# K projection of the last two chunks of layer 2 by Strassen, with its sums in free units of the h buffer

## The chip, the cores and the metric

The kernel runs on one core of one Trainium2 chip. The metric is the device time of one execution in microseconds; lower is better. The comparison uses the median of several executions.

## The reference

Four layers over a sequence of 2048 tokens of width 512: linear attention, feed-forward, linear attention, feed-forward, each with a layer norm in front and a residual behind. Both attention layers share their weights, and so do both feed-forward layers.

```python
def _A_ref(x, wqkv, wo):            # H = 32 heads of 16
    qkv = (x @ wqkv).reshape(B, S, 3, H, Dh).transpose(2, 0, 3, 1, 4)
    q, k, v = qkv[0], qkv[1], qkv[2]
    phi = lambda t: jnp.where(t > 0, t + 1, jnp.exp(t)) + 1e-6
    pq, pk = phi(q), phi(k)
    kv = jnp.einsum("bhsd,bhse->bhde", pk, v)
    z = jnp.einsum("bhsd->bhd", pk)
    num = jnp.einsum("bhqd,bhde->bhqe", pq, kv)
    den = jnp.einsum("bhqd,bhd->bhq", pq, z)[..., None] + 1e-6
    return (num / den).transpose(0, 2, 1, 3).reshape(B, S, D) @ wo

def _B_ref(x, w1, w2):              # Dff = 1376
    return jnp.maximum(x @ w1, 0) @ w2

x = x + _A_ref(_layernorm(x), wqkv, wo)
x = x + _B_ref(_layernorm(x), w1, w2)
x = x + _A_ref(_layernorm(x), wqkv, wo)
x = x + _B_ref(_layernorm(x), w1, w2)
```

## The kernel before

**Tiles and layers.** The sequence lies in 16 tiles of 128 tokens, and four tiles make a chunk, so there are chunks 0 to 3. The layers are numbered 0 to 3; layers 0 and 2 are attention, 1 and 3 feed-forward. `xn` holds the normed rows, `Tb` their transposes, which a DMA transpose on SP's queue (`tr8`, `tr10` and so on, two tiles each) writes from `xn`. `big` is one buffer of 44 units of 512 columns: in the feed-forward layers it holds the hidden activations h (unit `h_unit(c, t)`, 11 column blocks c for each chunk t), in the attention layers the phi of K (blocks 0 to 3) and of Q (blocks 4 to 7). Blocks 8 to 10 are not used by attention.

**Attention.** For each tile i, `kproj`i makes K with four matmuls of 512 columns; `a_k_proj` (line 590) sends the result through phi: two passes of ACT out of PSUM (`_lin`, `_exp`) and two of DVE (`_em`, `_phi`). `gacc`i then adds xn^T times phi(K) to an accumulator in four PSUM banks, `z`i the sums for the denominator. `qproj`t_j makes Q by column blocks of 128. `den`, `ln`, `rd` give the reciprocal denominators, which a DMA round trip spreads over the rows of `xn`; `us` multiplies them into phi(Q). `kvT`, `kvm`, `wp`, `wpe` make the small weight from the accumulator (copied out by `gev`), and `wo` the layer's output, which `resid` adds to the rows; `cen`, `sq` and the transposes lead to the feed-forward.

**Feed-forward.** Chunks 1 to 3 make h by one level of Strassen (products p1 to p7); the output products f1 to f7 and `fr` do so too, with the sums s1 to s4 of h on DVE. `q21`, `q22`, `r11`, `r12` pass partial results between those products, `residf` adds the output to the rows and sums them, `sq` (ACT) sums the squares, `mean`, `nm2`, `var`, `veps` (DVE), `rstd` (POOL) and `nbias` (DVE) make the norm's factors, `norm` (DVE or ACT) writes `xn`, `tr` transposes it into `Tb`.

**Strassen for Q.** In layer 2, chunk 3's Q is made by `a_str` (line 711): 512 tokens, 512 inputs and 512 outputs are halved each, and seven products of four 256-column matmuls take the place of sixteen 512-column matmuls. It needs five differences of weight blocks (`waq_0` to `waq_4`, line 686, in rows 8 to 12 of `xin`), four sums of blocks of `Tb` (`tb0` to `tb3`, line 703, in the chunk's own rows of `xn`), and between the products copies and additions of PSUM banks: `c6`, `c11`, `c12` (lines 747 and 748, ACT or DVE) and `c21`, `c22` (DVE). The products p1, p6 come first; p2 and p5 wait for c11, p3 and p4 for c21, p7 for c12.

**Order.** Nothing is scheduled on the chip. The program builds a list of operations with their dependences, and the table `ORDER` gives the order in which they are put into the engines' queues, with a letter that fixes the engine where there is a choice (a for ACT, d for DVE). `BANKS` gives each result's PSUM bank. Each engine works through its queue in order, and waits where an operand isn't there. So an operation that waits holds up everything behind it on its engine.

Of the kernel before, what the change touches and what calls it, by code (L numbers as in the profile page):

```python
# [9 lines left out]
F32 = mybir.dt.float32  # L10
# [123 lines left out]
49 37 45 50 73 38 46d 72 51 81 74 39a 75 52 54 82 76 53a 60 83 86 58 78 56 87 77 79 61 57 55 98 59 89 62 84 63 119 88  # L134
93 99 115 100 108 64 66d 95 65d 67a 103 80 69 117 68a 92 85 90 94 113 70 135 105 91 104 116 120 141 114 118 121 110
180 122 109 251 174 130 176 123 136 132 127d 124d 131 125d 142 138 126d 128 178 137 148 143 179 133 181 129 175 144
169 177 134 182 149 96 183 106 159 111 171 112 170 97 147 107 160 101 161 184 191 185d 186a 187d 139 164 140 150 189
172 192 153 173 165 151 239 188d 193 154 102 190 166 145 162 203 155 163 167 156 9 152 209 194 10 205 157 195 11 204
197 146 210 158 196 206 199 207 198 240 221 200 168 211 201 215 223 212 213 222 233 224 217 225 216 227 218 234 219
235 202 428 228 208 229 236 237 252 230 231 253 427 254 214 255 322 282 323 242 220 283 243 226 324 241 284 232 325  # L140
245 285 238 244 246 326 250 247 259a 329 248 249 257d 256a 260 286 258a 287 270 262 327 289 261 280 263 328 330 272
264 288 271 265 281 290 314 267 273 320 291 275 315a 333 331 321a 318 268 316 277 319d 294 317a 332 266 309 293 274
296 292 395 311 269 278 310 297 400 396 295 276 397 410 401 398a 279 405 402 411 403a 339 412 406 413a 415 334 407 340
408a 383 335 343 349 416 341 336 338 337d 344 350 342a 299 351 353 345 354 384 429d 304 346 352d 301 347d 433 300 424
355 434 436a 465 430d 306 466 449 425 435a 450 305 426 437 468a 438 385 356 298 421 312 451a 431d 386 470 348 432d 469
369 471d 439a 302 422d 399 371 307 423 303 404 377 372d 467a 414 389 440 363 388 378a 308 442 390 364a 313 441 472 387
443a 357 481 370d 444a 473 474 417 409 358 375 359 445 475a 476a 447 446 418 482 393 373 477 376a 392 365 483 394 448d
374a 484 367 452a 391 478 366a 419 498 368d 420 493 499 486 502 503 494 487 500 497 508 485 501d 495 488 504 496a 381
509 507 513 379 510 512 490 505 506d 479 511a 454 491 453 489 382a 514 515 360 380a 492 456 480a 519 361a 545d 455a
524 362 520 529 525 523 546d 566 528 534 567a 530 549 533 547d 458 550a 548d 603 459a 457 604a 598d 568 460a 599d 551  # L150
569 602 552 570 461 553 571 605a 463 554 572 462 464a 601d 555 535 573a 618 556a 674d 538 607 578 526 608a 675d 561
527a 600d 606 521 621d 522a 562 609 579 539 563 677d 557 574 564 580 558 581 565 678 559 575 679a 622 582 576 680 560
623 681 634 536 624a 583 682 637d 577 537d 610 683 638 613a 611 584 531 585 532d 639 612a 684 586 676d 540 587 640a
616 685a 614 695 617a 619 588 751d 696a 595 591d 620a 615 592a 697 625 690 596a 698 594 589a 627 516 590d 626 628a
752d 635 593 699 754d 636a 753d 629a 686 700 691 630 597 701 641 632 702a 631 642 517 541 633a 643 518 542 687 644d
692 707 645a 693 703 646 694 648 647 708 649a 688 755 803d 689 662 758a 804d 756 664 772 757a 805d 704 759 773a 709
806d 663 760 807 761a 705 650 808a 762 706 771 710 652 763 651 774d 809 711 712 764 766d 775 765a 810 769 665 713 811
770a 714 715 666 716 776 812 656 777a 778 717 813 719a 720d 780 814d 658 779 543 767 544 718a 819 653 781d 824 782a
722 787 654 657 815 783 825a 785 659 668 790d 786a 721d 792 768 670 723 791 793d 826 669 784 660 816 748 827 817 828
749a 671 818 788 829 724 750 789d 794 830 726 672 796 725 831d 795 820 797d 798a 727 832 728 836 799 837 800 801 730  # L160
802a 873d 736 732 731 874d 821 833 738 838 655 737 875d 877 876d 661 822 667 834 878a 823 839 879 835 894 880 840 673
895d 841 842 843 881 733 844 734 845 896 882 729 897 739 846 898 849d 850a 848d 883 847d 852 735 899 884d 900 740 851
1066 889 1065 890 1068 1067 885 901d 891 902 892 886 903 893 887 742 904 888 906 744 907 743 908 745 868 905 909 746
910 741 911 912 1069 869 747 913 914 870 915 858 871 872 943 916 860 920d 853 859 919d 861 922 958 855 862 918d 854
863 917d 959 856 921 960 944 857 865 948 961 864 962 953 866 950 867 949 933 951 954 952 955 968 935 956 934 928 957
936 937 969 930 929 923 931 932 938 924 925 945 939 970 926 940 927 963 941 942 980 965 964 946 966 982 971 967 981
947 983 972 984 985 973 995 974 987 975 1000 986 988 997 1001 989 996 1070 998 990 999 1071 978 1002 992 976 991 979
1005 993 1004 1072 1025a 977 1006 994 1003 1024a 1027 1023d 1026a 1073 1011 1029 1009 1047 1028 1030 1007 1012 1074
1048 1075 1077a 1010 1049 1013 1076d 1051 1078 1050a 1008 1053 1014 1055 1031 1054a 1032 1052d 1056d 1037 1034 1084
1033 1133 1039 1035 1015 1036 1038 1123 1017 1134 1018 1135 1118 1124 1016 1136a 1040 1128 1127 1125 1119 1126a 1019  # L170
1085 1120 1129 1042 1121a 1130 1022 1091a 1086 1138 1021 1044 1079 1020 1131d 1097 1043 1045 1182 1087 1139 1041 1046
1081 1167 1183 1080 1088 1184 1057 1168 1098 1172 1099 1169 1170d 1177 1058 1173 1137 1174 1147 1175d 1059 1100 1187
1082 1122 1149 1089 1090 1148a 1178 1159 1132 1060 1150d 1185a 1155 1179 1101 1180a 1083 1161 1092 1156a 1188 1196d
1151 1093 1162d 1094 1216 1189 1140 1152a 1063 1141 1200 1095 1171 1062 1096 1157 1142 1061 1203d 1160a 1143 1064
1219d 1106 1158a 1153 1107 1197d 1176 1163 1199d 1104 1154a 1165 1103 1108 1164d 1181 1201 1109 1102 1166a 1144 1105
1198d 1202a 1204 1300d 1186 1205 1207 1220 1145a 1232 1206a 1111 1193 1302d 1113 1235a 1217 1301d 1194a 1110 1208
1218a 1112 1209 1303d 1195 1236 1210a 1221 1223 1319 1222a 1146 1190 1248 1191 1117 1211a 1192 1115 1225 1114 1212
1224 1226a 1214 1116 1320a 1253 1213 1215a 1249 1321 1227a 1250 1251d 1237 1252 1258 1322 1254 1238a 1230 1255 1257
1323 1256d 1259 1231a 1263 1268 1324 1262 1304 1260 1264 1325 1265 1267 1261d 1233 1279 1305d 1326a 1266d 1234a 1228
1306 1269 1327 1307 1239 1330 1338d 1308 1280 1331 1309 1283 1241 1229 1240 1242d 1310 1243a 1281 1282a 1339d 1274  # L180
1311d 1244 1342 1275 1246 1343 1247a 1340d 1315 1345a 1245 1341d 1344a 1284 1390d 1278 1312 1285 1316 1391d 1288 1347
1276 1346 1392d 1277a 1358 1328 1349 1348a 1317 1294 1313 1332 1393d 1361a 1350 1351 1286 1333 1363 1352a 1362 1270
1364a 1271 1287d 1394 1353a 1272 1318 1273 1359 1329 1356 1360a 1289 1428d 1395a 1365 1357a 1396 1290 1366 1354 1335
1369a 1293 1397 1367 1291 1374 1336a 1292d 1398 1355 1368a 1295 1296 1372 1399 1375 1370 1377a 1400 1373a 1337 1379
1376d 1401a 1409 1371 1380a 1297 1405 1298 1314 1410a 1299 1402 1432 1411 1334 1429d 1435a 1431d 1378 1433 1412 1406
1430d 1434a 1413 1381 1437 1414 1382 1438a 1383 1415 1384a 1385d 1436 1416a 1386 1465 1403 1466a 1407 1387 1449 1404
1448 1450a 1439 1388 1420 1389a 1408 1451a 1421 1480d 1441 1440 1442a 1482d 1452 1443a 1464 1481d 1453 1467a 1417
1454a 1444 1446 1484 1447a 1445 1455 1422 1469 1485a 1468 1483d 1470a 1457 1418 1458a 1423 1499 1486 1471 1500a 1419
1456 1473 1487 1501 1424 1459a 1472 1474a 1502 1488 1460 1425 1461 1475a 1503 1489 1426a 1476 1462 1427 1490 1477
1463a 1504 1478 1517d 1491a 1505 1479a 1495 1506a 1515d 1496 1510 1516d 1497 1511 1498 1519 1518d 1534 1520a 1507  # L190
1535a 1521 1536 1522 1508 1537 1512 1523 1509 1538 1524 1492 1539 1513 1525 1540 1526a 1493 1541a 1530 1494 1527 1514
1528 1542 1529 1543 1545 1554 1544 1546 1531 1547 1555 1532 1548 1549 1533 1550 1551 1553 1552
"""
BANKS = ("0143601322754564754755774454754476476457623555746335427175640021331757302711647524361554634572435036"
# [1263 lines left out]
```

## Time and profile before

| | us |
|---|---|
| median of 5 runs | 271.37 |
| lowest, highest | 271.18, 271.56 |
| profiled execution | 271.37 |
| its span | 269.6 |
| PE, DVE, ACT busy in it | 263.1, 232.7, 196.0 |

The span runs from the first to the last instruction of the program; the profiled execution's time is 1.8 us longer. PE is the TensorE matmul, PEld the weight load beside it, DVE the VectorE, ACT the ScalarE, POOL the GpSimd, SP the SyncE that issues most DMAs. In a timeline each line has a start, a length, the engine, the source line, the operation with what it writes and reads, and, in brackets, idle time before it with what ended it. Line 539 is a helper that issues nearly all matmuls, so they are told apart by their operands: `ps<-wqkv,Tb` is a kproj, `ps<-Tb,wqkv` a qproj, `ps<-big,xn` a gacc, `ps<-gw,big` a wo, `ps<-xn,wqkv`, `ps<-xn,xin` and `ps<-Tb,xin` of 256 columns around 180 us are Q's Strassen products. The matmuls' ends are modelled, so rates are read from start to start. In the chain that ended last, each line has a start, a length and what the end of the execution waited for in that time.

### The profile page before, as it was taken

The numbers are of one execution on the slowest core, as the hardware profiler recorded it, in microseconds if no ns is written. First come the engines' busy times: TensorE is split into PE (matmuls) and PEld (weight loads), VectorE is DVE, ScalarE is ACT, GpSimd is POOL, SyncE is SP. The second block draws the span as 40 slices with busy tenths as digits, with TensorE's granted clock in tenths as the row PEclk, the third lists the DMA queues.
The fourth block names the chain that finished last, engine by engine and source line by source line (L and its number), as shares of the span: only waits on it lengthen the run. The fifth ranks groups of instructions, "written<-read, shape, count | busy, mean of one in ns | idle before, by whom it ended". The sixth has DMA issues, their size and how long they took to land.

```text
span 269.6 us, 5295 instructions
## 1 busy us (share of the span) xinstructions
PE 263.1 (98%) x1951; PEld 170.9 (63%) x1973; DVE 232.7 (86%) x635; ACT 196.0 (73%) x426; POOL 18.8 (7%) x30
## 2 busy tenths in 40 slices
PE   8999999999999999999999999999999999999995
PEld 2444454447556879778666544455458678888884
DVE  4999985999989999999799765599989999979875
ACT  3889956999978768787542887799998857657420
POOL 4111000000110002111010100000011001100000
PEclk9999999999999999999999999999999999999999
DMA  6954973254344026204004060215355222220204
GB/s 216 376 111 79 236 263 103 91 77 102 97 121 76 2 40 97 42 1 80 19 2 78 0 81 1 72 54 127 82 139 118 41 39 41 58 81 0 100 0 156
DMA packets 47481, 23.60 MB, mean 88 GB/s; under 512 B 36736, under 2 KB 46048, under 8 KB 47456
## 3 DMA queue, kind: packets, MB, share of 16 engines
q1 hardware_dynamic: 47312, 23.21, 35.1%
q8 instruction: 15, 0.25, 0.4%
q14 instruction: 10, 0.08, 0.1%
q10 hardware_dynamic: 144, 0.07, 0.1%
HBM read 11.21 MB, written 3.15 MB: 53 GB/s over the span
## 4 chain that ended last, share of the span: by engine, by line
PE 86%; DVE 9%; DMA 2%; issue 1%; ACT 1%
PE ps L539 84%; DVE bst L446 3%; DMA Tb<-xn 2%; PE ps L423 2%; DVE big L525 1%; DVE xn L478 1%; DVE xn L579 1%; DVE escr L523 1%; DVE mv L447 0%; PE ps L502 0%; DVE xin L1055 0%; ACT sqscr L546 0%; DVE escr L1055 0%; DVE xres L552 0%; DVE ps L1029 0%
## 5 line engine op out<-in xcount | busy, mean ns | idle before, releaser
L521 ACT ACTIVATE escr<-ps 128x512 bf16<-128x512 f32 x60 | 35.7, 606 | 8.0 <-PE ps L539 8.0
L546 ACT ACTIVATE sqscr<-xres 128x512 bf16<-128x512 f32 x48 | 30.4, 634 | 14.5 <-DVE xres L583 7.6
L519 ACT ACTIVATE big<-ps 128x512 bf16<-128x512 f32 x60 | 35.2, 608 | 1.0 <-PE ps L539 1.0
L1015 ACT ACTIVATE big<-ps 128x512 bf16<-128x512 f32 (+1 forms) x47 | 24.9, 536 | 9.6 <-PE ps L539 8.9
L539 PE MATMUL ps<-wqkv,Tb 128*128 128x512 bf16 x121 | 30.1, 379 | 1.2 <-DMA Tb<-xn 0.7
L539 PE MATMUL ps<-big,xn 128*128 128x512 bf16 x123 | 29.8, 379 | 0.3
L539 PE MATMUL ps<-gw,big 128*128 128x512 bf16 x120 | 28.7, 379 | 0.5
L539 PE MATMUL ps<-Tb,wqkv 128*128 128x512 bf16 x112 | 27.0, 379 | 0.1
L525 DVE TENSOR_TENSOR big<-big,escr 128x512 bf16<-128x512 bf16 x60 | 24.6, 421 | 2.4 <-ACT big L519 1.5
L523 DVE TENSOR_SCALAR escr<-escr 128x512 bf16<-128x512 bf16 x60 | 16.9, 288 | 9.5 <-ACT escr L521 9.0
L539 PE MATMUL ps<-w2s,big 128*128 128x256 f16 x160 | 21.9, 273 | 0.0
L539 PEld LDWEIGHTS ps<-wqkv,Tb 128*128 128x128 bf16 x128 | 12.0, 98 | 14.7 <-DMA Tb<-xn 1.2
L539 PEld LDWEIGHTS ps<-big,xn 128*128 128x128 bf16 x128 | 12.2, 98 | 13.7 <-issue 0.4
L539 PE MATMUL ps<-w,big 128*128 128x256 f16 (+2 forms) x113 | 20.6, 302 | 0.0
L539 PEld LDWEIGHTS ps<-gw,big 128*128 128x128 bf16 x128 | 12.2, 98 | 12.8 <-issue 0.5
L539 PE MATMUL ps<-w,xin 128*128 128x256 bf16 (+1 forms) x140 | 19.5, 273 | 0.0
L539 PE MATMUL ps<-xn,xin 128*128 128x256 f16 x128 | 19.5, 272 | 0.0
L998 ACT ACTIVATE ps<-ps 128x512 f32<-128x512 f32 (+1 forms) x28 | 14.6, 522 | 5.7 <-DVE big L1036 2.5
L539 PEld LDWEIGHTS ps<-Tb,wqkv 128*128 128x128 bf16 x112 | 10.8, 98 | 12.5 <-issue 0.2
L539 PE MATMUL ps<-xn,w 128*128 128x256 f16 x120 | 18.7, 273 | 0.0
L539 PE MATMUL ps<-Tb,w 128*128 128x512 bf16 x80 | 18.4, 379 | 0.0
L539 PE MATMUL ps<-Tb,wper 128*128 128x256 bf16 x120 | 18.3, 273 | 0.0
(152 smaller groups left out, 513.0 us busy)
## 6 DMA issues: line engine op xcount, KB each, us to landing
xn<-rdram SPq DMA_DIRECT2D x32, 128.0 KB
wqkv<-in_A_wqkv_dram SPq DMA_DIRECT2D x3, 512.0 KB, 7.2
xin<-in_A_x_dram SPq DMA_DIRECT2D x3, 512.0 KB, 8.0
out_dram<-xn SPq DMA_DIRECT2D x3, 512.0 KB, 2.6
w<-in_B_w_dram SPq DMA_DIRECT2D x1, 1376.0 KB, 6.4
w<-in_B_w_dram SPq DMA_DIRECT2D x1, 1280.0 KB, 9.8
rdram<-rsp SPq DMA_DIRECT2D x8, 128.0 KB, 1.7
wo<-in_A_wo_dram SPq DMA_DIRECT2D x1, 512.0 KB, 10.1
```

What stands on the lines that cost most here:

```text
L423: last = e.matmul(psv[:, wt, :], wrm[:, 0:128], wrm[:, :], start=True, stop=True)
L446: g.add(DVE, lambda e: e.bn_stats(bst[:, i, :], xin[:, i, :]), [("xin", i)] + list(behind), [("bst", i)], C_DVE_BNST, name="bnst%d" % i)
L478: (DVE, lambda e: e.tensor_scalar(xn[:, i, :], src, rstd[:, i:i + 1], nbias[:, i:i + 1], ALU.mult, ALU.add), C_DVE_NORM_BF if first else 4 ...
L519: g.add(ACT, lambda e: e.activation(dst_ap, psv[:, b, :], ACTF.Identity, bias=1.0 + 1e-6, scale=1.0), [("ps", b)], [dst_key], C_ACT_PSUM, ...
L521: g.add(ACT, lambda e: e.activation(escr[:, s, :], psv[:, b, :], ACTF.Exp), [("ps", b)], [("escr", s)], C_ACT_EXP, name=name + "_exp")
L523: g.add(DVE, lambda e: e.tensor_scalar(escr[:, s, :], escr[:, s, :], 1.0, 1e-6, ALU.min, ALU.add), [("escr", s)], [("escr", s)], C_DVE_BF4 ...
L525: g.add(DVE, lambda e: e.tensor_tensor(dst_ap, dst_ap, escr[:, s, :], ALU.max), [dst_key, ("escr", s)], [dst_key], 340.0, name=name + "_phi")
L539: last = e.matmul(o, l, r, start=st, stop=sp, skip_group_check=skip)
L546: g.add(ACT, lambda e: e.activation(sqscr[:, q, :], xres[:, i, :], ACTF.Square, accum_out=dst[:, i:i + 1]), [("xres", i)], [("sqscr", q), ...
L579: g.add(DVE, lambda e: e.scalar_tensor_tensor(xn[:, i, :], psv[:, b, :], rstdf[:, i:i + 1], xres[:, i, :], ALU.mult, ALU.add), rd, [("xn", ...
L998: g.add_flex([(ACT, lambda e: e.activation(dst(), psv[:, src, 0:W], ACTF.Identity), cost(C_ACT_PSUM)), (DVE, lambda e: e.tensor_copy(dst() ...
L1015: g.add_flex([(ACT, lambda e: e.activation(out_ap(r, m), pv(b), ACTF.Relu), cost(C_ACT_PSUM)), (DVE, lambda e: e.tensor_scalar(out_ap(r, m ...
```

## The change

K of chunks 2 and 3 of layer 2 is made by `a_str` as well (14 products in place of 8 groups of kproj). The five differences of K's weights lie in blocks 8 to 10 of `big` at chunks 0 and 1, the intermediate of c6 in blocks 8 and 9 at chunk 2, and the sums of `Tb` in the units that later take phi(Q) of the same chunk, because `xn` is still read by gacc. The differences are made new for each layer that needs them. The sums of `Tb` are no longer shared between kinds, so chunk 3 makes them twice, once for K and once for Q. The PSUM copies and additions are written as two halves of 256 columns for both kinds, since K's intermediate lies in two units.

`ORDER` and `BANKS` are new. The list grows from 1556 to 1585 operations; about twenty operations of other layers change between DVE and ACT, trev1 in the head and, at the end of layer 1, norm8 and norm13 to norm15 among them, and matmul groups stand in another order from the first layer on.

```diff
 17 0 14 12 15 18 13 1 16 19 2 20 22 3 24 4 21 23 25 5 6 26 27 7 28 8 29 40 30 33 31 32a 41 34 47 42 35 71 43 36 48 44
-49 37 45 50 73 38 46d 72 51 81 74 39a 75 52 54 82 76 53a 60 83 86 58 78 56 87 77 79 61 57 55 98 59 89 62 84 63 119 88
+49 37 45 50 73 38 46d 72 51 81 74 39d 75 52 82 56 76 53a 54 86 83 60 78 87 55 58 77 61 57 98 59 79 89 62 84 63 119 88
...
-                 ... QSTR=(3,), UACT=(), KSTR=(), GSPLIT=(15,), ...
+                 ... QSTR=(3,), UACT=(), KSTR=[(), (2, 3)], GSPLIT=(15,), ...
...
-        WSUM = {"q": 8, "k": 0}
...
         def qk_weight_sums(kind):
-            if kind in qk_sums:
-                return qk_sums[kind]
+            tag = kind, cur_layer[0]
+            if tag in qk_sums:
+                return qk_sums[tag]
...
-                i = WSUM[kind] + k
-                ap = xin[:, i, :].bitcast(F16).rearrange("p (c f) -> p c f", c=2)
-                keys = [("qks", kind, k), ("xin", i)]
+                if kind == "q":
+                    ap, own = xin[:, 8 + k, :], ("xin", 8 + k)
+                else:
+                    u = h_unit(8 + k % 3, k // 3)
+                    ap, own = unit_ap(u), ("big", u)
+                ap = ap.bitcast(F16).rearrange("p (c f) -> p c f", c=2)
+                keys = [("qks", kind, k), own]
...
-        def t_sums(t):
-            if t in t_sums_of:
-                return t_sums_of[t]
-            TS = [xn[:, 4 * t + k, :].bitcast(F16).rearrange("p (i c t) -> p i c t", c=2, t=128) for k in range(4)]
-            tk = [[("ts", t, k), ("xn", 4 * t + k)] for k in range(4)]
+        def t_sums(t, kind):
+            tag = t, kind, cur_layer[0]
+            if tag in t_sums_of:
+                return t_sums_of[tag]
+            home = [xn[:, 4 * t + k, :] if kind == "q" else unit_ap(pq_unit(k, t)) for k in range(4)]
+            TS = [x.bitcast(F16).rearrange("p (i c t) -> p i c t", c=2, t=128) for x in home]
+            tk = [[("ts", kind, t, k), ("xn", 4 * t + k) if kind == "q" else ("big", pq_unit(k, t))] for k in range(4)]
...
-            s6 = xin[:, 13:15, :].rearrange("p a b -> p (a b)").bitcast(F32)
-            k6 = [("xin", 13), ("xin", 14)]
+            if kind == "q":
+                s6 = xin[:, 13:15, :].rearrange("p a b -> p (a b)").bitcast(F32).rearrange("p (j k) -> p j k", k=256)
+                k6 = [("xin", 13), ("xin", 14)]
+            else:
+                s6 = big[:].bitcast(F32).rearrange("p (c t k) -> p c t k", t=NCH, k=256)[:, 8:10, 2, :]
+                k6 = [("big", h_unit(8, 2)), ("big", h_unit(9, 2))]
...
-                g.add_flex([(ACT, lambda e: e.activation(dst(), psv[:, src, :], ACTF.Identity), C_ACT_PSUM),
-                            (DVE, lambda e: e.tensor_copy(dst(), psv[:, src, :]), C_DVE_FLEX)],
+                g.add_flex([(ACT, lambda e: e.activation(dst(), pv(src), ACTF.Identity), C_ACT_PSUM),
+                            (DVE, lambda e: e.tensor_copy(dst(), pv(src)), C_DVE_FLEX)],
...
-                        if layer == 2 and t in KSTR:
+                        if t in KSTR[layer // 2]:
                             if i % 4 == 0:
                                 a_str(t, "k")
```

In the names of the prediction, `kp1_2` is K's product p1 of chunk 2 (p for product, and so on to `kp7_3`), `kc11_2` its copy c11, `wak_0` to `wak_4` the differences of K's weights, and `tb0_2`, `tb0_3` the sums of `Tb`.

## Prediction

> **What bounds the kernel now.** I read the page first, then the windows around the end of layer 1, then the chain that ended last, then the timelines of PE and DVE there.
>
> ```profile
> PE 263.1 (98%) x1951; PEld 170.9 (63%) x1973; DVE 232.7 (86%) x635; ACT 196.0 (73%) x426; POOL 18.8 (7%) x30
> PEclk9999999999999999999999999999999999999999
> PE 86%; DVE 9%; DMA 2%; issue 1%; ACT 1%
> ```
>
> PE is busy in 263.1 of 269.6 us at full granted clock, and 86% of the chain is PE. Of its 6.5 us of idle time most lies in the head and behind the last matmul. So a microsecond of matmul taken out anywhere in the middle is worth a microsecond, as long as PE finds its operands as early as before. That second condition is what this change strains, so I read the place where it acts.
>
> ```profile
> 135.00:150.00 15.00, 14.85 (x104) 9.87 (x104) 13.53 (x39) 6.24 (x17) 1.17 (x1) 1.00 0.19 36
> 150.00:160.00 10.00, 9.29 (x71) 4.51 (x71) 8.11 (x27) 8.22 (x19) 1.01 (x1) 1.00 0.46 55
> 160.00:168.00 8.00, 7.87 (x65) 4.03 (x65) 3.90 (x13) 5.79 (x12) 0.00 (x0) 1.00 0.00 1
> 168.00:178.00 10.00, 9.88 (x66) 4.97 (x66) 6.57 (x19) 8.34 (x17) 0.00 (x0) 1.00 0.20 67
> ```
>
> Columns: length, busy time of PE, PEld, DVE, ACT, POOL, clock, DMA. From 150 to 178 us DVE is idle for 9.4 us and ACT for 5.7; from 135 to 150 DVE has only 1.5 us left and ACT 8.8. The chain leaves PE in exactly one place of the middle:
>
> ```profile
> 149.53 0.04 DVE xres L583
> ...
> 150.32 0.72 ACT sqscr L546 x2
> ...
> 152.91 1.00 DVE xn L478 x2
> 153.91 0.03 DVE escr L523
> 153.94 4.74 DMA Tb<-xn
> 158.68 0.05 issue
> 158.72 3.84 PE ps L539 x17
> ```
>
> This is layer norm of chunk 3 between the layers: the last residual (residf13), its squares, the norm, the DMA transpose tr14, then kproj14. It takes 9.15 us from 149.53 to 158.68, and the work left for PE does not quite cover it:
>
> ```profile
> 156.18 1.89 PE L539 MATMUL ps<-Tb,wqkv 128*128 128x512 bf16 x8
> 158.72 1.04 PE L539 MATMUL ps<-wqkv,Tb 128*128 128x512 bf16 x4 [0.66 <-DMA Tb<-xn]
> ...
> 160.46 1.03 PE L539 MATMUL ps<-wqkv,Tb 128*128 128x512 bf16 x4
> 161.32 1.03 PE L539 MATMUL ps<-big,xn 128*128 128x512 bf16 x4
> ...
> 185.58 0.60 PE L539 MATMUL ps<-xn,xin 128*128 128x256 f16 x4
> 186.02 1.04 PE L539 MATMUL ps<-Tb,xin 128*128 128x256 bf16 x8
> ```
>
> PE idles 0.66 us before kproj14. The lines also give rates, from start to start: four matmuls of 512 columns (a kproj, qproj or gacc) take 0.86 us (160.46 to 161.32), one Strassen product of four 256-column matmuls takes 0.44 (185.58 to 186.02).
>
> **PE.** Over long runs the rates are finer: 24 matmuls of 512 columns from 190.78 to 195.96, 0.216 us each; ten of 256 columns from 139.72 to 140.81, 0.109 each. A chunk of K was 16 x 0.216 = 3.45 us and becomes 28 x 0.109 = 3.05. Two chunks: 0.80 us less, all of it on the path.
>
> The Trainium skill ("TensorE: Matmul & The Clock Gate", section "Back-to-back issue gap") speaks against the change: in a real stream with weight loads it gives about 81 ns per matmul at 128 columns and 131 at 512. A straight line between them is 98 ns at 256, and by that estimate a chunk would go from 2.10 to 2.75 us, 1.3 us lost over both. Weight loads (98 ns in the groups) do stay below 109 ns here and PE never runs a 512-column matmul in 131, so I use the rows.
>
> **DVE and ACT.** Added on DVE: five differences of K's weights (wak; four of Q's run from 144.24 to 145.58, 0.34 each), eight sums of T (tb, 0.34 in sequence), four additions out of PSUM (c21, c22, 0.69), one of six copies (0.69). Four norms of 0.46 (norm8, norm13 to norm15) move from DVE to ACT. That is 1.7 + 2.7 + 2.8 + 0.7 - 1.8 = 6.1 us. ACT gets five copies at 0.49 in sequence and four norms at 0.71: 5.3 us. The phi work is the same, eight pairs of ACT passes. Both sums fit under the idle times above, so I cost them at nothing as throughput; their cover is the 9.4 and 5.7 us, and if it went they would cost what exceeds it. What can hurt is position, since DVE and ACT run in order.
>
> **Position, before the transposes.** In the new order wak_1, waq_0 and wak_3 stand on DVE among the r11, q22, norm and residf steps of the last output pairs. Walking that queue with the durations above from s4_3 on, the four residuals come back to back, and residf13 starts about 0.5 us after its product fr0_13 is done, where it was 0.04. Behind it tb0_2 and wak_2 lie in the time that the squares of sq13 take anyway (var3 waits for them, 150.32 to 151.04). From nbias3 to the first transpose the new order (norm12 on DVE beside norm13 on ACT) takes about 1.0 us where two norms on DVE took 1.2. On SP's queue tr12 now goes before tr14, and POOL's rstd stands where it stood. Then kp1_3 needs tb0_3 behind the transpose: 0.42 and 0.05. So the chain from fr0_13 to kp1_3 is 0.5 + 9.15 - 0.2 + 0.47 = 9.9 us.
>
> The cover: between fr0_13 and kp1_3 the new order has gacc0 to gacc6 and the seven products of chunk 2, 7 x 0.86 + 7 x 0.44 = 9.1 us, where the old one had 8.6 (149.49 to 158.06). In there kp1_2 itself waits for tb0_2 behind residf13, by the same walk 0.2 us. So PE waits 9.9 - 9.1 - 0.2 = 0.6 at kp1_3, if the transpose again takes 4.74. The transposes of this trace go from 3.0 to 4.8 us (tr8 and tr10, the pair before, 3.1 and 3.2), unlike on equal work; with 3.2 the wait is nothing. I take the middle, 0.3: waits of 0.5 together where 0.66 was, 0.15 gained. Ends: 0.2 and 0.8, so 0.5 gained to 0.15 lost.
>
> **Position, the links.** In each chunk p2 and p5 wait for the copy c11, p4 and p3 for c21 (which waits for c6), p7 for c12. A link is 0.6 to 0.7 us of work and about 0.2 to see the matmuls end. PE work standing in each in the new order: chunk 2: kp6 and gacc2 (1.3), kp5, gacc3 and gacc4 (2.2), kp3 and gacc5 (1.3); chunk 3: gacc7 and kp6 (1.3), qproj0_1 (0.86), kp3 and three z sums (1.7). The thin one is qproj0_1. The Q chunk of the same form ran at 176.84 to 187.05 with no wait over 0.14. Behind the waiting DVE steps stand phi passes, for which gacc8 and later wait only microseconds afterwards. I take 0.1 for the links; ends 0 and 0.9.
>
> **The rest of the table.** About twenty engine choices swap between DVE and ACT in other layers; PE's list elsewhere has the same matmuls. Three spots I looked at. In the head trev1 moves to DVE, whose chain from 9.6 to 24 us is full: 0.35 us later transposes for chunk 2 of layer 0, but two more Q groups (1.7 us) stand before the K matmuls that need them, so nothing; 0.3 without that cover. At kvT, gev0 now follows the last gacc with two Q products (0.87) against 0.89 of need, at wo1 the copies wpe end about when PE arrives: 0.1 together, and the old 0.14 at wp1 goes. The tail has the same steps in another order. I take 0.15 for all; ends -0.2 and 0.6.
>
> **Sum.** The profiled execution took 271.37 us (span 269.6 and 1.8 around it), which is also the median of the runs, so no correction is needed. 271.37 - 0.80 - 0.15 + 0.1 + 0.15 = 270.67, said as 270.7. What this measurement can tell from no change is 0.2%, 0.54 us: faster begins below 270.83. The forecast is just beyond it.
>
> **Rivals.** *The boundary closes*: the transpose takes about 3.2, the 0.66 wait vanishes but for 0.2 at kp1_2, and the links cost nothing: 271.37 - 0.80 - 0.46 = 270.1. For it: the pair tr8, tr10 at 3.2; against it: the pair at this very place took 4.74 and 3.80. *The saving is eaten*: transposes at 4.8, links at 0.4, re-planned spots at 0.3: -0.80 + 0.15 + 0.4 + 0.3, 271.4. For it: DVE at 13.53 of 15 us just where three of the weight differences go. *Slower, by the links*: ACT is the busiest helper from 150 to 178 (22.4 of 28 us, near 27 with most of the additions), and if its queue puts each of the six links late, PE stands at each of them. It decides from 0.22 us per link: 6 x 0.22 = 1.34 us, the 0.80 saved and the 0.54 of the threshold. At 0.35 each, 2.1 us, the time is 271.37 - 0.80 + 2.1 = 272.7, or 272.5 with the boundary gain. Against it: five of six covers are 1.3 us or more, and all ACT's work there was 80% before.
>
> **How the numbers follow.** Forecast 0.45, boundary closes 0.15, eaten 0.25, slower by the links 0.15. The forecast's own range, by the ends of its terms, is 270.2 to 271.3; a fifth of it lies above 270.83, and nearly all of the eaten case lies within 0.2%. So faster 0.45 x 0.8 + 0.15 = 0.51, same 0.45 x 0.2 + 0.25 - 0.01 = 0.33, slower 0.15 and a little more, 0.16. The range from 270.0 to 271.9 takes in the first three cases and leaves out the last.
>
> **What would show it.** Right: Strassen products of K at 0.44 us from start to start; a wait of PE for DVE xn or big (the T sums) in place of the one for DMA Tb<-xn, together under 0.7 us; gacc groups without gaps. Residf13 should start some 0.5 us after its product. Wrong: several PE waits on ACT or DVE copies (L761 and L762 in the new file) of 0.2 or more between the transposes and den0; PE idle time beyond 7 us in all; or products slower than 0.44, which would make the matmul term itself false.

## Result, and the profile after

| | before | after |
|---|---|---|
| median, us | 271.31 (94 runs) | 270.62 (52 runs) |
| lowest, highest | 270.47, 274.64 | 270.07, 271.95 |
| profiled execution, its span | 271.37, 269.6 | 271.37, 269.5 |

The ratio is 0.9977 (95% interval 0.9971 to 0.9984): 0.69 us less by the medians, just beyond the 0.2% that can be told from no change, though the interval reaches down to 0.16%. The forecast was 270.7, in the range 270.0 to 271.9. That is close, but two of its terms missed, in opposite directions, so the closeness is in part luck.

The profiled execution of the kernel after took longer than most, and its page says why. These are its lines of busy time, clock and chain, and then all that PE waited for (total, times, longest):

```profile
PE 262.7 (97%) x1976; PEld 172.6 (64%) x1997; DVE 238.4 (88%) x650; ACT 199.2 (74%) x434; POOL 18.7 (7%) x30
...
PEclk9999999999999999999999999999999999999999
...
PE 94%; DMA 2%; DVE 1%; ACT 1%; issue 1%; SPq 0%
```

```profile
PE ps L424 <- DVE wrm L417: 1.2, 1, 1.2
PE ps L540 <- DMA wqkv<-in_A_wqkv_dram: 0.8, 1, 0.8
PE ps L540 <- DVE big L526: 0.3, 1, 0.3
PE ps L540 <- DVE Tb L511: 0.3, 1, 0.3
```

The load of the first weights landed at 7.59 us where it landed at 6.64 in the trace of before, so everything started 0.9 us later, and a wait of 0.3 in layer 0 came on top. A second profile of the same kernel (below) has neither, and took 270.23. What matters is that two lines are missing: no wait for a transpose, and none for the sums of `Tb`. DVE rose from 232.7 to 238.4 us, 5.7 where 6.1 were reckoned, and ACT from 196.0 to 199.2, 3.2 where 5.3 were reckoned.

The windows of the prediction, in the kernel after (length, busy time of PE, PEld, DVE, ACT, POOL, clock, DMA):

```profile
135.00:150.00 15.00, 14.89 (x110) 10.65 (x110) 14.57 (x48) 10.32 (x24) 2.12 (x2) 1.00 0.19 36
150.00:160.00 10.00, 9.95 (x107) 6.73 (x107) 9.23 (x27) 9.79 (x19) 0.00 (x0) 1.00 0.29 56
```

From 150 to 160 PE is busy for 9.95 us where it was 9.29. DVE has 0.4 and 0.8 us left in the two windows and ACT 0.2 in the second, so from 150 to 160 the idle time that covered the additions is nearly used up, and still PE doesn't wait. Its timeline at K's products of chunk 3, where the prediction looked for waits:

```profile
152.08 1.03 PE L540 MATMUL ps<-big,xn 128*128 128x512 bf16 x4
152.94 0.60 PE L540 MATMUL ps<-big,Tb 128*128 128x256 f16 x4
153.60 0.81 PE L540 MATMUL ps<-big,xn 128*128 128x512 bf16 x3
154.25 0.60 PE L540 MATMUL ps<-wqkv,big 128*128 128x256 bf16 x4
154.68 1.03 PE L540 MATMUL ps<-big,xn 128*128 128x512 bf16 x4
155.54 1.04 PE L540 MATMUL ps<-big,Tb 128*128 128x256 f16 x8
156.42 0.60 PE L540 MATMUL ps<-big 128*128 128x256 f16 x4
156.85 1.03 PE L540 MATMUL ps<-Tb,wqkv 128*128 128x512 bf16 x4
157.81 0.61 PE L540 MATMUL ps<-wqkv,big 128*128 128x256 bf16 x4
```

kp1_3 is the line at 154.25; no line carries an idle time in brackets. The first two lines are 0.86 us apart, kp6_3 and kp5_3 (the line at 155.54) take 0.88 together: 0.86 for four matmuls of 512 columns and 0.44 for a product, as forecast. One link shows, kp4_3 at 157.81, which starts 0.96 after qproj0_1 instead of 0.86. It is the link that the prediction called the thin one.

### The profile page after: what moved, and what is told of

Read it like the earlier page. It is cut to its first block, busy times and chain, and to the rows that moved or that the text cites. A ratio compares the mean times of both kernels' runs of the same rounds, so it can differ in the third digit from the quotient of the medians.

```text
span 269.5 us, 5363 instructions
## 1 busy us (share of the span) xinstructions
PE 262.7 (97%) x1976; PEld 172.6 (64%) x1997; DVE 238.4 (88%) x650; ACT 199.2 (74%) x434; POOL 18.7 (7%) x30
## 4 chain that ended last, share of the span: by engine, by line
PE 94%; DMA 2%; DVE 1%; ACT 1%; issue 1%; SPq 0%
PE ps L540 93%; DMA wqkv<-in_A_wqkv_dram 2%; ACT escr L522 1%; ACT big L520 0%; DVE big L526 0%; DVE xn L580 0%; DVE escr L524 0%; PE ps L503 0%; DVE Tb L511 0%; SPq L383 0%; DVE xn L1138 0%; SPq L385 0%
## 5 line engine op out<-in xcount | busy, mean ns | idle before, releaser
L522 ACT ACTIVATE escr<-ps 128x512 bf16<-128x512 f32 x52 | 30.7, 609 | 7.5 <-PE ps L540 7.2
L520 ACT ACTIVATE big<-ps 128x512 bf16<-128x512 f32 x52 | 31.0, 613 | 1.2 <-PE ps L540 1.1
L1027 ACT ACTIVATE big<-ps 128x512 bf16<-128x512 f32 (+1 forms) x44 | 22.9, 533 | 6.5 <-PE ps L540 5.7
L540 PE MATMUL ps<-wqkv,Tb 128*128 128x512 bf16 x91 | 22.7, 379 | 1.3 <-DMA wqkv<-in_A_wqkv_dram 0.8
L526 DVE TENSOR_TENSOR big<-big,escr 128x512 bf16<-128x512 bf16 x52 | 21.1, 421 | 1.5 <-ACT big L520 0.8
L524 DVE TENSOR_SCALAR escr<-escr 128x512 bf16<-128x512 bf16 x52 | 14.3, 286 | 4.3 <-ACT escr L522 4.2
L540 PEld LDWEIGHTS ps<-w2s,big 128*128 128x128 bf16 x160 | 15.5, 98 | 3.9 <-DVE xres L1105 0.4
```

What stands on the lines that cost most here:

```text
L520: g.add(ACT, lambda e: e.activation(dst_ap, psv[:, b, :], ACTF.Identity, bias=1.0 + 1e-6, scale=1.0), [("ps", b)], [dst_key], C_ACT_PSUM, ...
L522: g.add(ACT, lambda e: e.activation(escr[:, s, :], psv[:, b, :], ACTF.Exp), [("ps", b)], [("escr", s)], C_ACT_EXP, name=name + "_exp")
L524: g.add(DVE, lambda e: e.tensor_scalar(escr[:, s, :], escr[:, s, :], 1.0, 1e-6, ALU.min, ALU.add), [("escr", s)], [("escr", s)], C_DVE_BF4 ...
L526: g.add(DVE, lambda e: e.tensor_tensor(dst_ap, dst_ap, escr[:, s, :], ALU.max), [dst_key, ("escr", s)], [dst_key], 340.0, name=name + "_phi")
L540: last = e.matmul(o, l, r, start=st, stop=sp, skip_group_check=skip)
L1027: g.add_flex([(ACT, lambda e: e.activation(out_ap(r, m), pv(b), ACTF.Relu), cost(C_ACT_PSUM)), (DVE, lambda e: e.tensor_scalar(out_ap(r, m ...
```

## Where the time went: three stretches of PE

Executions differ in when the first weights land, so I compare PE from the first gacc group on. The columns: from there to f1_1 of layer 1; from f1_1 to the last part of gacc15 in layer 2, which holds the whole change; from there to the last fr0_13. The numbers are start times subtracted, in us. The rows with another number of warm-up matmuls are experiments told below.

| profile | to f1_1 | to gacc15 | to the end | sum |
|---|---|---|---|---|
| before | 73.39 | 90.38 | 92.02 | 255.79 |
| before again | 73.36 | 89.95 | 92.03 | 255.34 |
| before, 40 warm-ups | 73.38 | 89.54 | 92.03 | 254.95 |
| before, 40 warm-ups again | 73.43 | 89.54 | 92.03 | 255.00 |
| after | 73.72 | 89.15 | 92.00 | 254.87 |
| after again | 73.48 | 89.15 | 92.01 | 254.64 |
| after, 40 warm-ups | 73.24 | 89.35 | 92.00 | 254.59 |
| after, 40 warm-ups again | 73.37 | 89.36 | 92.11 | 254.84 |

Taking as the cost of each matmul group the median spacing of all groups with the same number and shape of matmuls, the matmuls of the last two stretches come to 180.84 us before and 180.06 after, 0.78 less. What lies above that, waits and gaps, is 0.73 us in the kernel before with 40 warm-ups (181.57 in all) and 1.10 in the kernel after (181.16).

The stretch "to gacc15" differs by 0.4 between two profiles of the same kernel before, and by 0.8 between the kernel before and one with other warm-ups. The experiments trace this to one transpose.

## Experiments

A ratio is to the kernel before, measured beside these runs, with its 95% interval. That kernel's median was 271.11 beside the first four runs, 271.40 beside the four with 40 and 25 warm-ups that come next, and 271.22 beside the last four.

**The same kernel after, again** (no edit).

> The changed kernel once more, unaltered, for a second profile of its head and for the chip on which the others run. If the late weight load in the head of its first profile (kproj0 waits 0.77 us for wqkv, all of PE 0.9 us later) belongs to that execution alone, kproj0 starts near 6.8 us as in the kernel before, and the profiled span is about 1 us below the kernel before's. If the new order causes it, kproj0 starts near 7.7 again. z12 should wait 0.3 us for k14_phi in both cases. Time: 0.6 to 0.8 us below the kernel before.

Measured: 270.32 (ratio 0.9973, 0.9963 to 0.9983); the profiled execution took 270.23, with a span of 268.3. The first weights landed in time and the wait of 0.3 in layer 0 shrank below 0.1. tr12 took 3.28, tr14 3.17. So the late start belongs to the first profile's execution, and the missing boundary wait to the kernel.

**K's first product twice.**

```diff
-                    return mms
+                    return mms * 2 if (kind, name) == ("k", "p1") else mms
```

It makes the products p1 of chunks 2 and 3 a second time, 8 matmuls of 256 columns.

> The changed kernel with product p1 of K issued twice in each of the two chunks, so that K's matmuls cost 2 x 0.44 = 0.87 us more and are as long as in the kernel before, while all of the added work of DVE and ACT stays. Theory 1 (PE sets the end, matmuls count in full): 0.87 us above the changed kernel. Theory 2 (DVE and ACT set the pace between the layers after the change): the extra matmuls fall into waits and cost under 0.3 us.

Measured: 271.10, 0.78 more than the kernel after on the same chip; the stretch to gacc15 grew by 0.87 (89.15 to 90.02), which is 8 x 0.109, and the other two stretches stayed within 0.1 of the second profile of the kernel after. Matmul time counts in full at this place.

**Before, with kproj7 behind fr0_13.** One group of 0.86 us more stands between the last output product and kproj14 (its phi, gacc7, z0 and kproj10 move with it).

```diff
-... 742 904 888 906 744 907 743 908 745 868 905 909 746
-910 741 911 912 1069 869 747 913 914 ...
+... 904 888 906 907 908 742 868 905 909 910 741 911 912
+1069 869 913 914 870 744 743 915 ... 943 859 919d 745 746 861 922 863 747 ...
```

> The kernel before with its plain K projection; one matmul group (kproj7) and what follows from it is moved from ahead of the last output products of layer 1 to behind them, so that the layer norm of chunk 3 starts 0.86 us earlier against PE's work. Theory 1 (the change has two gains, 0.80 us of matmuls and 0.66 us of the wait for the transpose): the wait before kproj14 goes, and the time falls by 0.4 to 0.7 us without any Strassen. Theory 2 (the wait is worth nothing, it comes back later as another one): the time stays within 0.2 us.

Measured: 271.21 (1.0009, 0.9999 to 1.0018), no gain. tr14 took 4.74 again. The wait for it went, but kproj10, kproj13 and kproj14 now waited for ACT (0.31, 0.22 and 0.12 start to start), and the stretch to gacc15 took 90.26. More cover by order alone traded one wait for three.

**After, with wa1_4 later on DVE** in layer 0, against the wait of 0.3 for `big` in the first profile.

```diff
-219 202 428 228 229 208 236 237 252 230 231 253 427 254 ...
+219 202 228 229 208 236 237 252 230 231 428 253 427 254 ...
```

> The changed kernel with the weight difference wa1_4 in layer 0, which stands on DVE and waits for the load of w1, moved behind k14_phi. Theory 1 (the wait of 0.34 us before z12 is DVE held up by that load): the wait goes and the time falls by 0.3 us. Theory 2 (k14_exp on ACT is what is late): the wait stays.

Measured: 270.72 (0.9991, 0.9971 to 1.0012). That wait went, as it had in the second profile without the edit, but its profiled execution, 271.30, waited 0.36 for `big` (L861) and 0.3 for `xres` behind DMAs that landed late in layers 0 and 2. Inconclusive: executions differ by more than the wait is worth.

**What made tr14 slow.** In all traces so far, packets of 16384 bytes on the instruction queue q8 came on average every 253 matmul and weight-load records of PE, and one fell into the slow transpose. These are GB/s in 40 equal slices and the packets on q8, first of the kernel before from 153 to 160 us, then of the kernel after from 148.5 to 155.5:

```profile
GB/s 0 0 0 0 0 0 0 0 0 0 0 0 132 211 206 255 26 0 0 0 0 7 9 10 9 44 282 288 274 288 290 293 287 181 0 0 0 0 47 0
...
q8 instruction: 1, 0.02, 0.8%
```

```profile
GB/s 0 0 0 0 0 0 0 0 0 0 0 0 0 0 110 222 221 217 212 197 186 122 114 219 224 197 217 202 215 96 26 0 0 0 0 0 0 0 0 0
```

In the kernel before, the two transposes start, the instruction packet comes at 155.8 us, and the flow drops from about 200 GB/s to 10 or less for 1.4 us (8 slices of 0.175). Afterwards it resumes faster than before. In the kernel after no q8 packet falls in, and the flow only dips between the two.

To move the packets without moving work, I wrote the 10 warm-up matmuls of the head as more and narrower ones, 40 of 128 columns or 25 of 200:

```diff
-                for k in range(WARM):
-                    last = e.matmul(psv[:, wt, :], wrm[:, 0:128], wrm[:, :], start=True, stop=True)
+                for k in range(40):
+                    last = e.matmul(psv[:, wt, 0:128], wrm[:, 0:128], wrm[:, 0:128], start=True, stop=True)
```

**Before, 40 warm-ups.**

> The kernel before, with its 10 warm-up matmuls of 512 columns in the head written as 40 of 128 columns: the same columns, 60 more PE instructions (30 weight loads and 30 matmuls), all in time in which PE waits for the first weights. Theory, fetch: in every trace so far a packet of 16384 bytes on the instruction queue q8 comes about every 256 PE instructions, and a transpose in whose run one falls 1.9 to 2.8 us after its issue takes 4.6 to 4.8 us instead of 3.0 to 3.4. 60 instructions more at the start bring each fetch some 4 us earlier, so the one at 155.8 us comes at about 152, before tr14 (153.94): tr14 and tr12 take 3.0 to 3.5, the wait of 0.66 at kproj14 goes, and the time falls by 0.2 to 0.6 to 270.7 to 271.1. Rival, place: tr14 is slow for where it stands (the pair of transposes, the traffic of that stretch); it takes 4.7 again, the wait stays and the time is that of before, 271.3 within 0.2.

Measured: 270.72 (0.9973, 0.9957 to 0.9990), 0.68 less than before. The packet came at 152.68, tr14 (issued 154.85) and tr12 took 3.10 each, and kproj14 follows the two groups ahead of it at 0.86 each, without a bracket:

```profile
157.09 1.89 PE L539 MATMUL ps<-Tb,wqkv 128*128 128x512 bf16 x8
158.82 1.03 PE L539 MATMUL ps<-wqkv,Tb 128*128 128x512 bf16 x4
```

The stretch to gacc15 fell by 0.84. This edit alone, with no Strassen for K, gains as much as the whole change. (The profiled execution itself took 271.54, because its first weights landed late, at 7.73 us; the stretches don't contain that.)

**After, 40 warm-ups.**

> The kernel after, with the same edit (40 warm-up matmuls of 128 columns). Theory, fetch: here the same 60 instructions bring the fetch from 156.7 us (first profile; 155.5 in the second) back into the run of tr12 and tr14 (148.7 and 150.1 to 153.3 in the second): they take 4.4 to 4.8 instead of 3.2 to 3.4, and since tb0_2 and tb0_3 arrived only 0.24 and 0.56 us before PE needed them, PE waits 0.5 to 1.2 us at kp1_2 and kp1_3 together: 270.8 to 271.5, as slow as the kernel before. Rival, place: transposes of 3.2 to 3.4, no wait, 270.3 to 270.6 as the kernel after.

Measured: 270.41 (0.9947, 0.9929 to 0.9965). The packet came at 151.75 and tr14 took 4.47, as the theory says, but the time is that of the kernel after: my 0.5 to 1.2 us of waiting were wrong. tr12 was nearly through (3.33), and kp1_3 needs only the sum tb0_3 of tr12's tiles. The first product to read tr14's tiles is kp6_3, one product and one gacc group later. It lost 0.2: it starts 1.06 us after gacc7 (153.45 to 154.51) instead of 0.86.

**After, 25 warm-ups**, meant as a control.

> The kernel after, with 25 warm-up matmuls of 200 columns (30 more PE instructions): the control of the edit itself. Theory, fetch: the fetch comes some 2 us earlier, at about 153.5 on the clock of the second profile, when tr12 is done and tr14 (150.1 to 153.25) has moved nearly all: both still take 3.2 to 3.5, and the time is that of the kernel after, 270.3 to 270.6. Were the smaller warm-up matmuls themselves what costs time, this run would be slower than the kernel after by a good part of what the run with 40 of them loses.

Measured: 271.25 (0.9997, 0.9979 to 1.0015), 0.8 slower than with 40. At the boundary all was as expected (3.31 and 3.18). But the first packet, at 18.06 us, now fell into tr4 of layer 0 (issued 15.04), which took 5.03, and the next K group waited for it:

```profile
18.47 0.54 PE L540 MATMUL ps<-ones,big 128*128 128x1 bf16 x16
20.12 1.25 PE L540 MATMUL ps<-wqkv,Tb 128*128 128x512 bf16 x5 [1.11 <-DMA Tb<-xn]
```

So it was no control, but a third place at which one packet costs PE a microsecond.

**Before, 25 warm-ups.**

> The kernel before, with 25 warm-up matmuls of 200 columns. Theory, fetch: the fetch of 155.8 us comes at about 153.5, just before tr14 is issued: tr14 takes 3.0 to 3.6, the wait of 0.66 shrinks to less than 0.2, and the time is 270.7 to 271.1, the same as with 40. Rival, place: tr14 at 4.7, the wait at 0.66, 271.3.

Measured: 271.22 (0.9978, 0.9961 to 0.9994). The packet came at 154.28, just before tr14 (154.36), which took 3.10; the boundary wait went (stretch 89.55). The other packet fell into tr4 in the head (4.43) and cost 0.4 there. My 270.7 to 271.1 had not followed the other packets.

**After, 48 warm-ups of 104 columns**, and one filler matmul less, to catch tr12.

> The kernel after, with 48 warm-up matmuls of 104 columns and one filler matmul less in the head: 74 more PE instructions. With 60 more, the fetch came at 151.75 us, 1.8 after tr14's issue: tr14 took 4.47 and PE lost 0.2 at kp6_3, which is the first to read tr14; kp1_3 needs only the sum of tr12's tiles and lost nothing. Theory, fetch: 14 instructions more bring it to about 150.9, 2.3 us behind tr12's issue (148.6): tr12 takes 4.4 to 4.8 instead of 3.3, tb0_3 is 0.6 to 0.9 us later than PE needs it, PE waits that long before kp1_3, and the time is 270.8 to 271.4. Rival, place: tr12 at 3.3, no wait there, 270.2 to 270.5 as with 40.

Measured: 271.14 (0.9991, 0.9979 to 1.0004). The packet came at 151.63, 2.7 us after tr12's issue: tr12 took 4.85 and tr14 4.35. Flow from 148 to 155 us, and PE at kp1_3:

```profile
GB/s 0 0 0 0 0 0 0 0 0 0 0 6 168 225 218 202 199 206 168 84 234 218 123 28 3 0 9 9 9 10 91 167 249 287 179 0 0 0 0 0
...
q8 instruction: 1, 0.02, 0.8%
```

```profile
152.49 1.03 PE L540 MATMUL ps<-big,xn 128*128 128x512 bf16 x4
154.27 0.61 PE L540 MATMUL ps<-wqkv,big 128*128 128x256 bf16 x4 [0.76 <-DVE big L710]
```

The flow of the kernel after now breaks as that of before did. kp1_3 waits 0.76 us for the sum of `Tb` (L710), and the gain is gone. The prediction's wait at kp1_3 exists; it needs a slow tr12.

**Before again** (no edit).

> The kernel before, unaltered, for a second profile. Theory, fetch: nothing moves PE's instructions, so the fetch of q8 comes at 155.5 to 156 us again, tr14 takes 4.5 to 4.8 and PE waits 0.5 to 0.8 before kproj14 again. Rival, chance: the slow transpose belonged to one execution; here it takes 3.0 to 3.5 and the wait is gone.

Measured: 271.23 (1.0005, 0.9988 to 1.0023). The packet came at 155.06, tr14 took 4.32 and PE waited for it:

```profile
158.22 1.04 PE L539 MATMUL ps<-wqkv,Tb 128*128 128x512 bf16 x4 [0.24 <-DMA Tb<-xn]
```

The wait is there again, at 0.24 instead of 0.66, below the 0.5 I had written; the packet came 1.2 us after tr14's issue, in the first profile 1.9. By the spacing of starts the two profiles show 0.40 and 0.82.

**Before and after, both with 40 warm-ups, again on one chip.**

> The kernel before with 40 warm-up matmuls again, for its median beside the kernel after with 40 on one chip: in neither does PE wait for a transpose at this place for more than 0.2 us, so their difference is what Strassen itself brings. By the matmul term alone (0.80) less 0.1 for the links it would be 0.7 us; by the two profiles (first matmul of gacc0 to the last fr0_13: 254.95 and 254.60) and the medians (270.72 and 270.41) it is 0.3 to 0.4. Expected: 270.6 to 270.9.

> The kernel after with 40 warm-up matmuls again, beside the one above: 270.2 to 270.5, 0.3 to 0.4 under it if more than half of the gain was the fetch; 0.6 or more under it if the matmul term comes out in full.

Measured: before 270.76 (0.9975, 0.9964 to 0.9986), after 270.59 (0.9972, 0.9961 to 0.9983). In the first pair the difference was 0.31, and the intervals overlap by 0.0008; here it is 0.17, and the two intervals lie almost on each other. So with the boundary clear in the one and nearly clear in the other (0.2 at kp6_3), the medians hardly tell the change itself from no change.

The stretches tell it better, since they leave out the head. Where no slow transpose makes PE wait at the boundary, the last two stretches together take 181.57, 181.57 and 181.58 us in three profiles of the kernel before (two with 40 warm-ups, one with 25), and 181.15, 181.16 and 181.15 in three of the kernel after (two with 10, one with 25). The change itself is worth 0.41 us there. With 40 warm-ups the kernel after takes 181.36 and 181.47, so only 0.2 and 0.1 of it is left, in keeping with the small differences of the medians.

## Why the prediction was right or wrong

**PE, -0.80: right.** It was 0.78 by the spacing of the matmul groups, and the doubled product shows that each 0.109 counts. The rule of the Trainium skill ("TensorE: Matmul & The Clock Gate", section "Back-to-back issue gap") that spoke for a loss of 1.3 us doesn't hold in this stream: four 512-column matmuls stay at 0.86 and four of 256 at 0.44.

**Boundary, -0.15: the mechanism half right, the size wrong.** I saw that the transposes ranged from 3.0 to 4.8 us "unlike on equal work", did not ask what those above 4 us share, and took the middle. The cause was in the trace of before. In the 14 profiles there are 420 of these transposes. A q8 packet starts 1.0 to 2.9 us after issue in 35 of them: 25 take 4.2 to 4.9 us, the other 10 take 3.0 to 3.1. In those 10 it comes at 2.5 us or later, but so it does in eight of the slow ones; four of the 10 stood in the traces from which I wrote that every transpose with a packet at 1.9 to 2.8 us was slow. Of the other 385 the median is 3.17 and four exceed 4.2; the longest, 5.03 (tr4 with 25 warm-ups), has a packet 3.0 us after its issue. In the kernel after, tr12 and tr14 are issued at 148.7 and 150.1 us (second profile) where it was 155.6 and 153.9, while the packet comes at 155.5, much as before, and so it misses them. Nothing in the plan aimed at that, so this part of the gain is luck. By the kernel before with 40 warm-ups against the kernel before as it is, it is worth 0.68 and 0.46 us of median; the term failed by 0.3 to 0.5. The walk along DVE was too gloomy as well: residf13 started 0.24 us after its product ended, not 0.5, and kp1_2 waited for nothing where 0.2 was reckoned.

**Links, +0.1: right.** Only qproj0_1 is too thin, and kp4_3 loses 0.09.

**Rest of the table, +0.15: too small.** The waits and gaps of the two later stretches grew by 0.37 (0.73 to 1.10), of which the link takes 0.09. In the rest, 0.28, are new gaps of 0.08 to 0.11 us at kvT, qp4_3, wo12 and two places of layer 3's feed-forward, less three that went, and differences too small to place. And the wait of 0.14 at wp1 that I booked as a gain was none: the record of wp0 is missing there in the first profile of before; the second shows wp0 in its place, 0.07 late. The number behind this term was off too: by the two ORDER tables not about twenty but 49 operations that both kernels have change between DVE and ACT, 26 of them to ACT and 23 to DVE.

**Sum.** -0.78 + 0.09 + 0.28 is -0.41 for the change with a clear boundary on both sides (the two later stretches go from 181.57 to 181.16), and another 0.4 to 0.8 comes from the packet that misses. In the sum column the two profiles of before and the two of after differ by 0.8 on average, and the medians by 0.7 to 0.8: the first stretch, 0.2 longer in the profiles of after, takes some of it back. So 270.7 came out near 270.62 because errors cancel: the boundary gave 0.3 to 0.5 more than its term, while the rest of the table cost 0.13 more and the first stretch 0.2. The "own range" of 270.2 to 271.3 also isn't what the ends of the terms add up to; that would be 269.9 to 272.2, which is wider than the stated range on both sides. Of the rivals, "boundary closes" came true in its mechanism; "eaten" came half true for what the Strassen products earn by themselves (0.41 left of 0.78), though not by slow transposes. The slow links did not come, although ACT ran at 9.79 of 10 us.

What stays open: why the pair's flow stops for 1.4 us around a packet that itself took 0.92 us there, and why a packet 2.5 us or more after issue slows some transposes and not others. The runs with other warm-ups show that the slow transposes follow PE's instruction packets; no run tells whether they wait for the packet or for something beside it.

## What to carry to other kernels

When the same DMA takes 3 us here and 5 there, look for what falls into the longer of them before taking a mean; the packets by queue in that window answer it from the trace of before. And before crediting a gain of a few tenths of a per cent to an edit, compare it with the same kernel with a few dozen idle PE instructions added in the head: they shift every later instruction packet and cost nothing by themselves (with 40 warm-ups the first K group started at 6.79 and 6.80 us in three of four profiles, as in the two of the kernel before; in the fourth the weights were late). Even then, follow all the packets, for one moved out of a bad place may land in another.

## What the runs showed of the hardware

PE's instructions arrive by DMA in packets of 16384 bytes on q8, at about every 253 records: 60 more PE instructions in the head brought the packet at 155.8 us to 152.7, and a sixteenth packet where there were 15. The Trainium skill ("Runtime: NRT & Kernel Launch", section "Instruction fetch mechanics") tells of blocks of 16 KiB with 256 instructions, mostly hidden. Size and spacing agree with the traces. PE itself shows no stall at them either: the kernel before's stretch to gacc15 takes 89.54 to 89.55 us in three profiles though the packet near the boundary comes at 152.7, 152.5 and 154.3. But a DMA transpose under way takes up to 1.9 us longer (5.03 where the median is 3.17), and PE then waits up to 1.1 us for its result.

The load of the first weights lands at different times in different executions of the same program: at 6.40 and 7.59 us in two of the kernel after, which moves the start of the first K group from 6.53 to 7.73, and at 5.96 and 7.73 in two of the kernel before with 40 warm-ups.
